# Cross attention and two fp32 MLPs on one core: where the next batch's x, the parts of V and one batch of products stand in the first MLP's steps

## The chip, the core and the metric

The kernel runs on one core of a Trainium2 chip. Five engines matter: TensorE (PE; its weight loads are listed apart as PEld), VectorE (DVE), ScalarE (ACT), GpSimd (POOL) and SyncE (SP), which here does nothing but issue DMA transfers. The metric is the device time of one execution in microseconds (us).

## The reference

Eight batches of attention, and two MLPs over all the tokens of the result. Everything is float32.

```python
B, H, S, Ns, D = 8, 8, 512, 32, 64          # x: (B,H,S,D), state: (B,H,Ns,D)
a  = softmax(x @ state.T / sqrt(D))          # per batch and head, S x Ns
xread = a @ state                            # S rows
a2 = softmax(state @ x.T / sqrt(D))          # Ns x S
sread = a2 @ x                               # Ns rows
X = concat([xread, sread]) -> (B*(S+Ns), H*D) = 4352 x 512
# MLP 1: w_in 512 x 2048, w_out 2048 x 512
h = X @ w_in
g = where(h >= 1, h, where(h <= -1, 0, (h + 1)**2 / 4))
Y = g @ w_out
# MLP 2: its own w_in, w_out of the same sizes, and a slope alpha per hidden unit
h2 = Y @ w_in2
out = (max(h2, 0) + alpha * min(h2, 0)) @ w_out2
```

## The kernel before, in words

A product of float32 matrices is made as a sum of three products of a rounded type: each operand is split into a high part and a rest (names ending in `h` and `l`), and high by high, rest by high and high by rest are added up in one PSUM bank. ACT makes the high part (a cast, L73), DVE the rest (a subtraction, L76).

**The first MLP's steps.** The tokens of batch t make tile t (t = 0 to 7, 512 columns); tile 8 holds the 256 rows of sread. Hidden units come in 16 blocks of 128. One *step* i is one (tile, block) pair; `gi(t, f)` is the number of the step of tile t and block f, so tile 1 is steps 16 to 31, tile 7 is steps 112 to 127. In the turn of step i the source has, one behind the other: the cast and the rest of g of step i+1 (`g_split`: ACT `gh`, DVE `gl`); the side work that tables hang on that step (`at(i, ...)`); `h_mm(i+2)`, the six products that make the hidden block two steps ahead in a PSUM bank `hA` (L84); its activation (ACT `y` L549 and L550, DVE `g` L552); `out_mm(i)`, twelve products into four banks `accA` (L584); and the work hung behind them (`by(i, ...)`). The side work of a tile is the attention of the *next* batch, the decoding of weights for the second MLP, and, in tile 7, the first of the second MLP's inputs. The second MLP (`second()`, lines from L700 on) follows tile 8.

**V.** xread @ w_in is not formed from xread: since xread = a @ state, the kernel makes V = state @ w_in once per batch (PE `vgp`, L460, four batches at a time as a group; ACT copies them to `vgo`, L463), writes V to DRAM (`vd<-vgo`, L475, `vg_store`), and reads each batch's V back in eight parts of 256 KB (`vr_load`, L481: `vr<b><block><half>`). Each part is split: ACT `vw...h` (`vr_hi`, L73), DVE `vw...l` (`vr_lo`). `h_mm` multiplies these by the attention weights `ath` and `atl` (the split of `at`, which the attention of that batch makes). Part (block blk, half q) of batch b is cast by ACT at step o = t0 + 10 + 4 blk + q, t0 being the first step of the tile *before* batch b's own; `vr_load` was hung on o - 2.

**x for the scores.** The scores of batch b are made in tile b-1, from t0 on: `ld_x1` loads x in an order that DVE can transpose (`s0`, L152), `s2_all` multiplies (PE `sc`, L179, at step t0 + 2), then softmax in stages `s3` to `s9` (L189 to L203 and on), with PE transposes `et` (L203). For b > 1 each half q of a batch is 8 transfers of 64 KB, 32 partitions of 128-byte pieces (L130), all hung on one step, t0 + q - 4, into two tiles of 2 KB a partition.

**Who decides the order.** All loads in question go through one queue, SP's, in its order. An engine executes its instructions in the order of its list; that list is laid out ahead of time by a scheduler that takes, among the instructions it believes ready, the one that stands first in the source. So TensorE's list is not the source's: an instruction whose inputs the scheduler holds for late is passed by later ones. Tiles in SBUF come from pools in turn: `U` has 72 buffers of 2 KB a partition, `V` 14 buffers of 4 KB; a load into a buffer that is still read waits, at the head of SP's queue, and what stands behind it waits too. In PSUM four banks serve `hA`, `vgp`, `sc` and `et` in turn, four serve `accA`.

Where the functions below begin with `at` or `by`, the first argument is the step.

Of the kernel before, what the change touches and what calls it, by code (L numbers as in the profile page):

```python
# [40 lines left out]
def kernel_body(ctx: ExitStack, tc: tile.TileContext, x, state, w1i, w1o, w2i, w2o, alpha, out):  # L41
# [9 lines left out]
    def U(name, dt=F32):  # L51
        return up.tile([128, 512], dt, tag="u", name=name)

    def V(name, dt=F32):
        return vp.tile([128, 1024], dt, tag="v", name=name)
# [7 lines left out]
    act, dve, pool, pe, ld = nc.scalar, nc.vector, nc.gpsimd, nc.tensor, nc.sync  # L63

    def run(*calls):


        gens = [g for g in (fn(*a) for fn, *a in calls) if g is not None]
        while gens:
            gens = [g for g in gens if next(g, gens) is not gens]  # L70
# [32 lines left out]
    A = {}  # L103
# [12 lines left out]
            op=ALU.mult)  # L116
        BD[b] = f

    def ld_x1(b, q):
        A[b, q] = {}  # L120
        if b == 1:
            t = A[b, q]["x1"] = V(f"x1_{b}{q}")
            ld.dma_start(out=t, in_=x[b, 4 * q:4 * q + 4].rearrange("h (s r) d -> (h s) (r d)", r=16))
            return
        A[b, q]["x1"] = [U(f"x1_{b}{q}{u}") for u in range(2)]
        for u, t in enumerate(A[b, q]["x1"]):
            for h in range(2):
                for e in range(2):
                    p = 64 * (h ^ q) + 32 * e
                    ld.dma_start(out=t[p:p + 32].rearrange("s (r i) -> s r i", i=32),  # L130
                                 in_=x[b, 4 * q + 2 * u + h, :, 32 * e:32 * e + 32].rearrange("(r s) i -> s r i", s=32))

    def ld_x2(b, q):
# [8 lines left out]
    def s0(b, q):  # L142
        a = A[b, q]
        x1 = a.pop("x1")
        a["xt"] = []
        for e in range(2):
            t = U(f"xt{b}{q}{e}")
            if b == 1:
                dve.transpose(out=t.rearrange("p (s r) -> p r s", r=16),
                              in_=x1.rearrange("p (r e i) -> p r e i", e=2, i=32)[:, :, e, :])  # L150
            else:
                dve.transpose(out=t, in_=x1[e])  # L152
            a["xt"].append(t)
            yield

# [185 lines left out]
    def first_back(q):  # L341
# [4 lines left out]
        a["at"] = ps  # L346

    STAGES = [s0, None, s2, s3, s4, s5, s6, s7, s8, s9]

    W = {}  # L350
# [163 lines left out]
    steps = [(t, f) for t in range(NB + 1) for f in range(NF)]  # L514

    def gi(t, f):
        return t * NF + f
# [6 lines left out]
    def h_mm(i):  # L524
        t, f = steps[i]
        n = wd_(t)
        blk, c = f // 4, (f % 4) * 128
        fs = slice(c, c + 128)
        ps = PS(f"hA{t}{f}")
        if t < NB:  # L530
            terms = []
            for q in range(2):
                vh, vl = VW[t, blk, q]
                ah, al = aT[t, q]
                terms.append((vh[:, fs], vl[:, fs], ah, al))
        else:
            terms = [(W["w1s", blk, k][0][:, fs], W["w1s", blk, k][1][:, fs],
                      XS["h"][:, k * 256:(k + 1) * 256], XS["l"][:, k * 256:(k + 1) * 256]) for k in range(4)]
        mm3(ps[:, :n], terms)
        HP[i] = ps  # L540
# [25 lines left out]
    def out_mm(i):  # L566
        t, f = steps[i]
        n = wd_(t)
        if f == 0:
            for k in range(NO):  # L570
                ACC[k] = pa.tile([128, 512], F32, tag="acc", name=f"accA{t}{k}")
        if i < NAT:

            g, w = GH.pop(i), G["dec", ("w1o", f)]
            for k in range(NO):
                pe.matmul(ACC[k], w[:, k * 128:(k + 1) * 128], g, start=(f == 0), stop=(f == NF - 1))  # L576
            return out_end(i)
        gh, gl = GH.pop(i)
        wh, wl = W["w1o", f]
        for k in range(NO):  # L580
            ks = slice(k * 128, (k + 1) * 128)
            prods = ((wh[:, ks], gh[:, :n]), (wh[:, ks], gl[:, :n]), (wl[:, ks], gh[:, :n]))
            for j, (a, b) in enumerate(prods):
                pe.matmul(ACC[k][:, :n], a, b, start=(f == 0 and j == 0), stop=(f == NF - 1 and j == 2))  # L584
        out_end(i)
# [380 lines left out]
    side = defaultdict(list)  # L966
# [3 lines left out]
    def at(i, fn, *a):  # L970
        side[i].append((fn, *a))

    def by(i, fn, *a):
        behind[i].append((fn, *a))
# [31 lines left out]
    for b in range(1, NB):  # L1006
        t0 = gi(b - 1, 0)
        for q in range(2):
            o = t0 + 4 * q
            n = o if b == 1 else t0 + q - 1  # L1010
            at(n - 2 - (b > 1), ld_x1, b, q)
            at(o + 3, ld_x2, b, q)
            for k, s in enumerate(STAGES):
                if s is s2 and b > 1:
                    if q:
                        at(t0 + 2, s2_all, b)
                elif s:
                    at((n if k == 0 else t0 + q if k == 3 and b > 1 else o) + k, s, b, q)
        for blk in range(4):
            for q in range(2):  # L1020
                o = t0 + 10 + 4 * blk + q
                at(o - 2, vr_load, b, blk, q)
                at(o, vr_hi, b, blk, q)
                at(o + 1, vr_lo, b, blk, q)

# [4 lines left out]
    for blk in range(4):  # L1030
        for c in range(4):
            if blk:
                o = 4 * blk + 1 + c
                at(o, vg_mm, 0, blk, c)
                at(o + 2, vg_store, 0, blk, c)
                o = gi(1, c) if blk < 2 else 4 * blk - 7 + c
                by(o, vg_mm, 1, blk, c)
                if blk > 1:
                    by(o, v0_move, blk, c)
                    if c % 2:  # L1040
                        by(o + 1, vr_hi, 0, blk, c // 2)
                        by(o + 1, vr_lo, 0, blk, c // 2)
                at(o + 2, vg_store, 1, blk, c)
            at(gi(1, 4 * blk + c - 4), wi_store, blk, c)

    for blk in (1, 2, 3):
        for c in range(4):
            o = 4 * blk - 7 + c - (blk > 1)
# [3 lines left out]
    for f in range(1, NF):  # L1052
        o = f - 2 - (f >= NAT)
        at(o - 3, d_load, ("w1o", f), src_w1o(f))
        decode(("w1o", f), o)
    for f in range(NF):
        o = gi(1, f - 3) if f < NAT else f - 2
# [73 lines left out]
    st_build(0)  # L1131
    st_build(1)
    run((s9, 0, 0), (s9, 0, 1), (dec1, ("w1o", 0)))
    for i in range(min(side), len(steps)):
        todo = [(g_split, i + 1)] if 0 <= i + 1 < len(steps) else []
        if i in (-4, -3):
            h_mm(i + 4)
            todo.append((act_fn, i + 4))
        todo += side.pop(i, [])
        if 0 <= i < len(steps) - 2:  # L1140
            h_mm(i + 2)
            todo.append((act_fn, i + 2))
        run(*todo)
        if i >= 0:
            out_mm(i)
        run(*behind.pop(i, []))
    second()


# [27 lines left out]
```

## Time and profile before

| what | us |
|---|---|
| median of 3 runs | 1371.51 (1370.38 to 1373.39) |
| the profiled execution, its own time | 1371.31 |
| its span in the trace | 1369.4 |
| PE busy in the span | 1336.7 |
| tile 1 of the first MLP | 82.57 |
| tiles 2 and 5 | 69.11 and 69.13 |
| tiles 4 and 6 | 72.23 and 72.98 |
| tile 7 | 66.47 |

The span is the stretch of the trace from the first to the last instruction; the execution's own time holds 1.9 us more around it. A tile's time is from its first product into `accA` to that of the next tile. Tiles 1 to 6 have the same arithmetic on PE but for the four pairs of `vgp` products that stand in tile 1 (18 more PE records than in tile 2); tile 7 has no attention to make for a further batch.

### The profile page before, as it was taken

How to read it: one execution, taken by the hardware profiler on the slowest of the kernel's cores; microseconds unless marked ns; L12 is line 12 of the kernel's file. 1: busy time of each engine (PE TensorE's matmuls, PEld its weight loads, DVE VectorE, ACT ScalarE, POOL GpSimd, SP SyncE). 2: the span in 40 equal slices, each digit the busy share in tenths (PEclk: the TensorE clock that was granted, in tenths of full speed). 3: DMA queues.
4: the chain of work that ended last, by engine and by line, in shares of the span. 5: the costliest groups of instructions: out<-in, count | busy, mean ns of one | idle time of the engine just before them, and what ended most of it. 6: DMA issues, size and time to landing. Idle time of an engine off the chain costs nothing.

```text
span 1369.4 us, 20766 instructions
## 1 busy us (share of the span) xinstructions
PE 1336.7 (98%) x6936; PEld 1108.2 (81%) x6936; DVE 1024.9 (75%) x1849; ACT 779.2 (57%) x1500; POOL 75.2 (5%) x94
## 2 busy tenths in 40 slices
PE   6999999999999999999999999999999999999998
PEld 3345668787878787888987888888889999999998
DVE  6897464868777877976978796787858777796873
ACT  4667765666666755766665454444635545464552
POOL 0010000011101120211200000000000000000000
PEclk9999999999999999999999999999999999999999
DMA  6978842265585647376467676656687888869875
GB/s 227 339 241 282 221 132 55 70 162 173 146 229 151 194 125 196 127 244 215 148 223 279 215 277 197 232 155 218 212 258 267 283 286 297 275 239 286 266 263 179
DMA packets 279370, 293.82 MB, mean 215 GB/s; under 512 B 136160, under 2 KB 170208, under 8 KB 279264
## 3 DMA queue, kind: packets, MB, share of 16 engines
q1 hardware_dynamic: 271680, 282.08, 64.8%
q10 hardware_dynamic: 7072, 9.37, 2.1%
q0 software_dynamic: 512, 1.05, 0.3%
q8 instruction: 55, 0.90, 0.3%
q14 instruction: 51, 0.42, 0.1%
HBM read 224.53 MB, written 66.06 MB: 212 GB/s over the span
## 4 chain that ended last, share of the span: by engine, by line
PE 85%; DVE 6%; DMA 5%; ACT 2%; issue 1%; SPq 0%; ACTq 0%; DVEq 0%
PE accB L825 24%; PE hB L750 22%; PE accA L584 21%; PE hA L84 12%; DMA vr<-vd 3%; PE vgp L460 2%; PE accA L576 1%; DMA xr<-xd 1%; PE sr L252 1%; DVE g L552 1%; DMA w1d<-wu 1%; DMA wr_wi<-in_moe_w_in_dram 0%; PE et L203 0%; DMA st<-in_state_dram 0%; DVE c L759 0%
## 5 line engine op out<-in xcount | busy, mean ns | idle before, releaser
L825 PE MATMUL accB<-gs,wv 128*128 128x384 f32 (+1 forms) x1680 | 332.1, 356 | 0.9 <-ACT o L843 0.9
L825 PEld LDWEIGHTS accB<-gs,wv 128*128 128x128 f32 x1680 | 300.9, 188 | 27.5 <-ACT o L843 1.6
L750 PE MATMUL hB<-xh,wu 128*128 128x384 f32 (+1 forms) x1120 | 315.6, 357 | 2.8 <-DVE m L759 1.2
L750 PEld LDWEIGHTS hB<-xh,wu 128*128 128x128 f32 x1120 | 205.7, 188 | 23.6 <-ACT p L776 2.2
L750 PE MATMUL hB<-xl,wu 128*128 128x384 f32 (+1 forms) x560 | 199.6, 356 | 0.0
L73 ACT CAST gs<-c 128x384 fp32r<-128x384 f32 (+1 forms) x200 | 109.3, 557 | 76.3 <-PE accB L825 55.8
L552 DVE SCALAR_TENSOR_TENSOR g<-y,hA 128x512 f32<-128x512 f32 (+1 forms) x144 | 93.6, 650 | 67.1 <-ACT y L550 66.7
L757 ACT ACTIVATE m<-c 128x384 f32<-128x384 f32 (+1 forms) x120 | 68.2, 568 | 118.7 <-DVE c L772 109.3
L76 DVE TENSOR_TENSOR gl<-g,gh 128x512 fp32r<-128x512 f32 (+1 forms) x135 | 93.9, 695 | 47.5 <-ACT gh L73 46.7
L549 ACT ACTIVATE y<-hA 128x512 f32<-128x512 f32 (+1 forms) x144 | 82.5, 573 | 69.2 <-PE hA L84 69.0
L76 DVE TENSOR_TENSOR gs<-c,gs 128x384 fp32r<-128x384 f32 (+1 forms) x200 | 114.6, 603 | 4.4 <-ACT gs L73 3.7
L759 DVE SCALAR_TENSOR_TENSOR c<-m,beta_sb,c 128x384 f32<-128x384 f32 (+1 forms) x120 | 80.9, 674 | 46.5 <-ACT m L757 44.1
L750 PEld LDWEIGHTS hB<-xl,wu 128*128 128x128 f32 x560 | 105.1, 188 | 8.7
L73 ACT CAST gh<-g 128x512 fp32r<-128x512 f32 (+1 forms) x135 | 80.2, 594 | 45.3 <-DVE g L552 37.0
L550 ACT ACTIVATE y<-y 128x512 f32<-128x512 f32 (+1 forms) x144 | 87.5, 608 | 3.8
L799 DVE TENSOR_TENSOR c<-c,c 128x384 f32<-128x384 f32 (+1 forms) x120 | 71.8, 608 | 1.9
L772 DVE TENSOR_TENSOR c<-hB,u 128x384 f32<-128x384 f32 (+1 forms) x80 | 48.5, 606 | 16.5 <-PE hB L750 9.1
L76 DVE TENSOR_TENSOR gs<-m,gs 128x384 fp32r<-128x384 f32 (+1 forms) x80 | 47.1, 608 | 16.4 <-ACT gs L73 16.4
L73 ACT CAST gs<-m 128x384 fp32r<-128x384 f32 (+1 forms) x80 | 43.4, 556 | 24.5 <-PE accB L825 21.1
L463 ACT COPY vgo<-vgp 128x512 f32<-128x512 f32 x64 | 34.8, 588 | 32.2 <-PE vgp L460 31.8
L460 PE MATMUL vgp<-wf_wi,sts 64*128 64x512 f32 x128 | 42.7, 640 | 4.8 <-DVE g L552 3.0
L838 DVE TENSOR_TENSOR c<-accB,o 128x384 f32<-128x384 f32 (+1 forms) x30 | 18.2, 608 | 35.9 <-PE accB L825 28.4
(907 smaller groups left out, 2563.4 us busy)
## 6 DMA issues: line engine op xcount, KB each, us to landing
wu<-w1d SPq DMA_DIRECT2D x280, 256.0 KB
wv<-w2d SPq DMA_DIRECT2D x280, 256.0 KB
vr<-vd SPq DMA_DIRECT2D x56, 256.0 KB
w1d<-wu SPq DMA_DIRECT2D x56, 256.0 KB
w2d<-wo SPq DMA_DIRECT2D x40, 256.0 KB
x<-in_x_dram SPq DMA_DIRECT2D x18, 512.0 KB
wr_wi<-in_moe_w_in_dram SPq DMA_DIRECT2D x16, 512.0 KB
wr_w1o<-in_moe_w_out_dram SPq DMA_DIRECT2D x16, 512.0 KB
```

Of the source, the lines that this page charges most:

```text
L73: act.copy(h, raw)
L76: (eng or dve).tensor_tensor(out=l, in0=raw, in1=h.bitcast(F32), op=ALU.subtract)
L84: pe.matmul(ps, a, b, start=(k == 0), stop=(k == n - 1))
L460: pe.matmul(ps[u], ST[g][rows, c * 128:(c + 1) * 128], w[rows], start=True, stop=True)
L549: act.activation(out=y[:, :n], in_=ps, func=AF.Relu, bias=0.5, scale=0.5)
L550: act.activation(out=y[:, :n], in_=y[:, :n], func=AF.Square)
L552: dve.scalar_tensor_tensor(out=g[:, :n], in0=y[:, :n], scalar=1.0, in1=ps, op0=ALU.min, op1=ALU.max)
L584: pe.matmul(ACC[k][:, :n], a, b, start=(f == 0 and j == 0), stop=(f == NF - 1 and j == 2))
L750: pe.matmul(ps, a[:, kk], b, start=(new and m == 0), stop=(m == 5), skip_group_check=True)
L759: dve.scalar_tensor_tensor(out=g, in0=m, scalar=beta_sb[:, f:f + 1], in1=h, op0=ALU.mult, op1=ALU.add)
L799: dve.tensor_tensor(out=o, in0=x, in1=y, op=op)
L825: pe.matmul(ps, a[:, js], b, start=(new and k == 0 and n == 0), stop=(k == 7 and n == 2), skip_group_check=True)
```

## The change

Four things change. First, x for the scores goes into one tile of 4 KB a partition per half (pool `V`) in place of two of 2 KB (pool `U`), and its transfers, the same 16 per batch of the same 64 KB, hang four a step on steps t0 - 6, t0 - 5 (half 0), t0 - 4, t0 - 3 (half 1), in place of eight on t0 - 4 and eight on t0 - 3. Second, each of V's parts is loaded at o - 3 in place of o - 2. Third, the products that make V of the second group of batches for blocks 0 and 1 (of those hung on `by`, block 1: `vgp110` to `vgp117`) move from behind steps 16 to 19 to behind steps 21 to 24, all in tile 1, and their stores to DRAM with them. Fourth, from step 16 to step 125 TensorE's list is that of the source; the other engines' lists, and TensorE's before and after, are still laid out by the scheduler.

```diff
--- before.py
+++ after.py
@@ -116,18 +116,18 @@
             op=ALU.mult)
         BD[b] = f
 
-    def ld_x1(b, q):
-        A[b, q] = {}
+    def ld_x1(b, q, us=(0, 1)):
+        if 0 in us:
+            A[b, q] = {"x1": V(f"x1_{b}{q}")}
+        t = A[b, q]["x1"]
         if b == 1:
-            t = A[b, q]["x1"] = V(f"x1_{b}{q}")
             ld.dma_start(out=t, in_=x[b, 4 * q:4 * q + 4].rearrange("h (s r) d -> (h s) (r d)", r=16))
             return
-        A[b, q]["x1"] = [U(f"x1_{b}{q}{u}") for u in range(2)]
-        for u, t in enumerate(A[b, q]["x1"]):
+        for u in us:
             for h in range(2):
                 for e in range(2):
                     p = 64 * (h ^ q) + 32 * e
-                    ld.dma_start(out=t[p:p + 32].rearrange("s (r i) -> s r i", i=32),
+                    ld.dma_start(out=t[p:p + 32, u * 512:u * 512 + 512].rearrange("s (r i) -> s r i", i=32),
                                  in_=x[b, 4 * q + 2 * u + h, :, 32 * e:32 * e + 32].rearrange("(r s) i -> s r i", s=32))
 
     def ld_x2(b, q):
@@ -149,7 +149,7 @@
                 dve.transpose(out=t.rearrange("p (s r) -> p r s", r=16),
                               in_=x1.rearrange("p (r e i) -> p r e i", e=2, i=32)[:, :, e, :])
             else:
-                dve.transpose(out=t, in_=x1[e])
+                dve.transpose(out=t, in_=x1[:, e * 512:e * 512 + 512])
             a["xt"].append(t)
             yield
 
@@ -1008,7 +1008,11 @@
         for q in range(2):
             o = t0 + 4 * q
             n = o if b == 1 else t0 + q - 1
-            at(n - 2 - (b > 1), ld_x1, b, q)
+            if b == 1:
+                at(o - 2, ld_x1, b, q)
+            else:
+                for u in range(2):
+                    at(t0 - 6 + 2 * q + u, ld_x1, b, q, (u,))
             at(o + 3, ld_x2, b, q)
             for k, s in enumerate(STAGES):
                 if s is s2 and b > 1:
@@ -1019,7 +1023,7 @@
         for blk in range(4):
             for q in range(2):
                 o = t0 + 10 + 4 * blk + q
-                at(o - 2, vr_load, b, blk, q)
+                at(o - 3, vr_load, b, blk, q)
                 at(o, vr_hi, b, blk, q)
                 at(o + 1, vr_lo, b, blk, q)
 
@@ -1033,7 +1037,7 @@
                 o = 4 * blk + 1 + c
                 at(o, vg_mm, 0, blk, c)
                 at(o + 2, vg_store, 0, blk, c)
-                o = gi(1, c) if blk < 2 else 4 * blk - 7 + c
+                o = gi(1, 5 + c) if blk < 2 else 4 * blk - 7 + c
                 by(o, vg_mm, 1, blk, c)
                 if blk > 1:
                     by(o, v0_move, blk, c)
@@ -1131,7 +1135,7 @@
     st_build(0)
     st_build(1)
     run((s9, 0, 0), (s9, 0, 1), (dec1, ("w1o", 0)))
-    for i in range(min(side), len(steps)):
+    def step(i):
         todo = [(g_split, i + 1)] if 0 <= i + 1 < len(steps) else []
         if i in (-4, -3):
             h_mm(i + 4)
@@ -1144,6 +1148,14 @@
         if i >= 0:
             out_mm(i)
         run(*behind.pop(i, []))
+
+    for i in range(min(side), gi(1, 0)):
+        step(i)
+    with tc.manual_schedule(engines={mybir.EngineType.PE}):
+        for i in range(gi(1, 0), gi(8, -2)):
+            step(i)
+    for i in range(gi(8, -2), len(steps)):
+        step(i)
     second()
```

SP's list around the loads of V's parts for batch 4, block 2 (`vr420`, the half 0), in tile 3. `x1_...` are the loads of x for the scores of batch 5, `w2d` are stores of decoded weights, `x2_50` is x for another stage. Before:

```order
L481 DMA vr410_3594<-vd0_1_81 128x1x512
L130 DMA x1_500_3596<-in_x_dram 32x16x32 x4
L130 DMA x1_501_3597<-in_x_dram 32x16x32 x4
L481 DMA vr411_3644<-vd0_1_81 128x1x512
L130 DMA x1_510_3646<-in_x_dram 32x16x32 x4
L130 DMA x1_511_3647<-in_x_dram 32x16x32 x4
L650 DMA w2d_90<-wo30_3660 128x512
L650 DMA w2d_90<-wo32_3737 256x1x256 x2
L650 DMA w2d_90<-wo33_3795 256x1x256 x2
L137 DMA x2_50_3914<-in_x_dram 128x16x64
L481 DMA vr420_3784<-vd0_2_82 128x1x512
```

The stretch of the same queue up to the same load with the change:

```order
L130 DMA x1_50_3485<-in_x_dram 32x16x32 x4
L650 DMA w2d_90<-wo22_3453 256x1x256 x2
L130 DMA x1_51_3603<-in_x_dram 32x16x32 x2
L481 DMA vr410_3555<-vd0_1_81 128x1x512
L130 DMA x1_51_3603<-in_x_dram 32x16x32 x2
L481 DMA vr411_3601<-vd0_1_81 128x1x512
L650 DMA w2d_90<-wo23_3501 256x1x256 x2
L357 DMA wr_w2o_8_3616<-in_moe2_w_out_dram 128x512
L130 DMA x1_51_3603<-in_x_dram 32x16x32 x4
L650 DMA w2d_90<-wo30_3654 128x512
L357 DMA wr_w2o_9_3726<-in_moe2_w_out_dram 128x512
L481 DMA vr420_3723<-vd0_2_82 128x1x512
```

The 16 loads of x stood in two blocks right ahead of `vr411` and, with five stores, of `vr420`; now they are spread in pieces of two to four over a longer stretch, ten of them ahead of the part `vr410` (four of these before the rows shown).

TensorE's list in tile 1 at the first of the four pairs of `vgp` (the last `accA` product of a step, the pair, the next hidden block). Before, behind step 16:

```order
L584 MATMUL accA13_1569<-gl16_1492,w_w1o_0h_1388 128x512
L584 MATMUL accA13_1569<-gh16_1491,w_w1o_0l_1390 128x512
L460 MATMUL vgp110_1582<-wf_wi_1_0_396,sts1_368 128x512
L460 MATMUL vgp111_1583<-wf_wi_1_0_396,sts1_368 128x512
L84 MATMUL hA13_1590<-ath10_1030,vw100h_1166 128x512
L84 MATMUL hA13_1590<-atl10_1032,vw100h_1166 128x512
```

With the change, behind step 21:

```order
L584 MATMUL accA13_1571<-gl21_1733,w_w1o_5h_1643 128x512
L584 MATMUL accA13_1571<-gh21_1732,w_w1o_5l_1645 128x512
L460 MATMUL vgp110_1809<-wf_wi_1_0_396,sts1_368 128x512
L460 MATMUL vgp111_1810<-wf_wi_1_0_396,sts1_368 128x512
L84 MATMUL hA18_1817<-ath10_1032,vw120h_1626 128x512
L84 MATMUL hA18_1817<-atl10_1034,vw120h_1626 128x512
```

The pair itself is unchanged; it now stands five steps later, ahead of the hidden block of step 24 in place of that of step 19, as `h_mm` runs two steps ahead. The three other pairs move alike.

DVE's list in tile 7. `xr001` is an addition of two tiles of the second MLP's input (L711, it needs the four loads `xr<-xd`), `gl120` the rest that the second product of step 120 needs, `vw730l` and `vw731l` rests of V's parts. Before:

```order
L552 SCALAR_TENSOR_TENSOR g120_6306<-y120_6307,hA78_6285 128x512
L76 TENSOR_TENSOR vw730l_6294<-vr730_6216,vw730h_6292 128x512
L76 TENSOR_TENSOR gl120_6341<-g120_6306,gh120_6340 128x512
L711 TENSOR_TENSOR xr001_6542<-xr011_6544,xr001_6542 128x1024
L552 SCALAR_TENSOR_TENSOR g121_6345<-y121_6346,hA79_6325 128x512
L76 TENSOR_TENSOR vw731l_6335<-vr731_6253,vw731h_6333 128x512
```

With the change:

```order
L552 SCALAR_TENSOR_TENSOR g120_6296<-y120_6297,hA78_6275 128x512
L76 TENSOR_TENSOR vw730l_6284<-vr730_6169,vw730h_6282 128x512
L711 TENSOR_TENSOR xr001_6532<-xr011_6534,xr001_6532 128x1024
L76 TENSOR_TENSOR gl120_6331<-g120_6296,gh120_6330 128x512
L552 SCALAR_TENSOR_TENSOR g121_6335<-y121_6336,hA79_6315 128x512
L76 TENSOR_TENSOR vw731l_6325<-vr731_6208,vw731h_6323 128x512
```

The addition `xr001` has moved ahead of `gl120`; the rest of the order stands.

## Rows read from the trace of the kernel before

**Rows 1.** The page: engine, busy us, share of the span, instructions.

```profile
PE 1336.7 (98%) x6936; PEld 1108.2 (81%) x6936; DVE 1024.9 (75%) x1849; ACT 779.2 (57%) x1500; POOL 75.2 (5%) x94
```

**Rows 2.** Windows of PE, tiles 1, 2, 4, 6, 7: us, busy, clock, DMA.

```profile
158.39:240.96 82.57, 79.01 (x395) 0.98 0.46 127
240.96:310.07 69.11, 69.11 (x377) 1.00 0.43 117
...
379.33:451.56 72.23, 69.93 (x378) 1.00 0.68 184
...
520.69:593.67 72.98, 70.63 (x377) 1.00 0.61 183
593.67:660.14 66.47, 65.84 (x307) 1.00 0.62 203
```

**Rows 3.** Waits of PE in tiles 1, 4, 6, 7: us, times, longest.

```profile
PE vgp L460 <- DVE g L552: 3.0, 2, 1.9
PE accA L584 <- ACT oA L595: 0.5, 1, 0.5
...
PE et L203 <- DVE g L552: 1.8, 1, 1.8
...
PE et L203 <- ACT e L195: 2.4, 1, 2.4
...
PE accA L584 <- DVE gl L76: 0.6, 1, 0.6
```

**Rows 4.** Timeline of ACT: start, us, instruction, idle before and its releaser.

```profile
181.67 0.62 ACT L73 CAST vw121h<-vr 128x512 fp32r<-128x512 f32 x1 [3.02 <-DMA vr<-vd]
...
392.09 0.62 ACT L73 CAST vw420h<-vr 128x512 fp32r<-128x512 f32 x1 [5.79 <-DMA vr<-vd]
...
532.39 0.62 ACT L73 CAST vw620h<-vr 128x512 fp32r<-128x512 f32 x1 [3.58 <-DMA vr<-vd]
```

**Rows 5.** Timeline of SP's queue, tiles 3 and 4, ahead of `vr420`.

```profile
362.35 6.92 SPq L130 DMA_DIRECT2D x<-in_x_dram  x8
...
370.03 6.68 SPq L130 DMA_DIRECT2D x<-in_x_dram  x8
...
381.92 2.83 SPq L481 DMA_DIRECT2D vr<-vd  x1
```

**Rows 6.** Timeline of SP's queue, tile 1, from `vr121` on.

```profile
171.42 4.17 SPq L481 DMA_DIRECT2D vr<-vd  x1
...
177.14 9.16 SPq L475 DMA_DIRECT2D vd<-vgo  x5
```

**Rows 7.** Timeline of PE, a `vgp` pair in tile 1.

```profile
168.07 1.13 PE L460 MATMUL vgp<-wf_wi,sts 64*128 64x512 f32 x4
169.13 0.50 PE L84 MATMUL hA<-ath,vw110h 128*128 128x512 f32 x1
```

**Rows 8.** Window of PE behind the last `vgp` wait, columns as rows 2.

```profile
186.56:189.98 3.42, 3.42 (x11) 0.50 0.47 136
```

**Rows 9.** Timeline of PE, the scores in tile 6.

```profile
527.23 1.04 PE L179 MATMUL sc<-xt,sts 64*32 64x512 f32 x2
528.20 0.50 PE L584 MATMUL accA<-gl,w_w1o_1h 128*128 128x512 f32 x1
```

**Rows 10.** Timeline of DVE and of PE, tile 7, around step 120.

```profile
621.72 0.69 DVE L76 TENSOR_TENSOR gl<-g,gh 128x512 fp32r<-128x512 f32 x1 [0.78 <-ACT gh L73]
627.52 1.23 DVE L711 TENSOR_TENSOR xr<-xr,xr 128x1024 f32<-128x1024 f32 x1 [5.11 <-DMA xr<-xd]
...
626.54 0.39 PE L584 MATMUL accA<-gl,w_w1o_8h 128*128 128x512 f32 x1
```

**Rows 11.** Timeline of DVE and of PE, the edge of tiles 5 and 6.

```profile
508.69 1.22 DVE L76 TENSOR_TENSOR atl<-at,ath 128x512 fp32r<-128x512 f32 x1
...
508.45 0.39 PE L84 MATMUL hA<-ath,vw600h 128*128 128x512 f32 x1
508.68 0.39 PE L84 MATMUL hA<-atl,vw600h 128*128 128x512 f32 x1
```

## The prediction

> **What bounds the kernel now.** I read the page first, and there TensorE: it is busy for 1336.7 us of the 1369.4 us span [rows 1]. Nothing that only makes another engine faster can pay; time is to be had where TensorE stands still, works at half clock, or switches between kinds of products. The next view is therefore windows of TensorE tile by tile [rows 2]. Tile 2 takes 69.11 us and has no idle time: that is what a tile of this arithmetic costs. Tile 4 takes 72.23 us, tile 6 72.98, tile 1 82.57, of which tile 1 has more to do (four pairs of `vgp` products). So 3.12 us are lost in tile 4, 3.87 in tile 6, and in tile 1 something of 13.46. Third, who it waits for there [rows 3]: two `vgp` products of tile 1 wait 3.0 us in all, the transposes `et` wait 1.8 us in tile 4 and 2.4 us in tile 6, each time for `g` on DVE or `e` on ACT. These are small instructions on engines that are far from full, so the fourth view is what held those engines up: ACT, just before, stood for 3.02 us at the cast `vw121h`, 5.79 us at `vw420h` and 3.58 us at `vw620h`, each time for a part of V to arrive [rows 4]. ACT runs its list in order: behind a blocked cast stand the casts `gh`, the activations `y` and the exponentials `e` of the scores, thus DVE's `g` and `gl`, thus the PSUM bank that a `vgp` or `et` needs. The last view says why the part is late. SP spends 6.92 and 6.68 us on two blocks of x for the scores, and the load of `vr420` only comes at 381.92, its cast being wanted at 386.3 (392.09 less the 5.79 of idle time) [rows 4, 5]. In tile 1 the queue is full of stores of V: `vr121` is issued at 171.42 and arrives ten microseconds later, amid five stores that take 9.16 us [rows 6].
>
> **x earlier and thinner, V's parts a step earlier.** No byte and no transfer is added; 16 transfers a batch stay. What moves is their place in SP's list. I counted there, for each part, the steps between the last wait ahead of it in the queue and its cast. A step is 18 products 0.23 us apart (the two starts in [rows 11]), about 4.1 us. For `vr420` the count goes from 3.7 to 4.7, for `vr120` and `vr121` from 3.0 to 5.0 and 4.0, for `vr620` and `vr621` from 1.7 and 2.7 to 4.6 and 3.7. The ACT stalls of 3.02, 5.79 and 3.58 us [rows 4] are 0.7, 1.4 and 0.9 of a step, and for `vr420` the 13.6 us of x in the way are gone besides [rows 5]. So I take these stalls as gone. In tile 4 this gives back all of the 3.12 us over tile 2; the low bound is the 1.8 us of the wait itself [rows 2, 3]. In tile 6 it gives the 2.4 us of wait [rows 3]. The buffer of 4 KB in place of two of 2 KB costs nothing: the transposes read the same 512 columns, and in the list no load of x waits for a reader of its new buffer; its cover is the 6 to 18 steps between issue and transpose, and if a buffer were late, x would stand at the queue's head as before.
>
> **TensorE in source order.** In tiles 1 to 7 the lists differ in three ways. At the tile edges the scheduler had let the first hidden blocks of the next tile pass ahead of `out_mm` in pieces; that order had no wait, and the new one has none unless the attention weights are late, which is a rival below: 0. The scores of tile 6 stood in two pieces with products of another kind between; the first piece holds TensorE for 0.97 us (528.20 less 527.23 [rows 9]), and I take the two pieces to cost one such stretch more than one piece will: 0.9 us. With the wait of 2.4 that makes 3.3 of tile 6's 3.87; the rest is slower restarts that go with them, and I take 3.87, bounds 2.4 and 3.87. The `vgp` pairs move, and each keeps its price: 1.06 us from the pair to the next product [rows 7], about 1.3 with the slower product on each side. Four make 5.2 us, before and after.
>
> **Tile 1.** Of the 13.46 us over tile 2, 5.2 are the pairs, which stay. 3.0 are the two waits [rows 3]; they go, because the casts `vw120h` and `vw121h` no longer hold up ACT, and because the pairs now stand behind step 21, past those casts. Right behind the second wait TensorE shows a granted clock of 0.50, the lower of its two levels, for 3.42 us [rows 8]: at the upper one the same work is 1.71 us, so 1.71 are lost, and go with the wait. 0.5 is a wait for the copy of tile 0's result [rows 3], which stays. The remaining 3.0 (13.46 less 5.2, 3.0, 1.71 and 0.5) are slow starts around these places; I take 1.2 of them as going. Together 5.9; bounds 4.7 (waits and clock alone) and 7.8 (all but the pairs and the 0.5).
>
> **Tile 7, a cost.** DVE's list puts the addition `xr001` ahead of `gl120`. Before, it stood behind it and waited 5.11 us for its loads, and started at 627.52 [rows 10]; TensorE ran on and lost 0.6 us a step later [rows 3]. The loads have no reason to come sooner. So `gl120` would start at 627.52 + 1.15, end near 629.2, and the second product of step 120, at 626.54 before [rows 10], would wait 2.7 us; the 0.6 behind it goes. That would be +2.1; the loads and DVE's turn may shift by some tenths, and I take +1.4, bounds 0 and +3.8 (2.1 and half clock once more at the price of [rows 8]).
>
> **The sum.** −5.9 − 3.1 − 3.9 + 1.4 = −11.5. The profiled execution took 1371.31 us, span and 1.9 us around it, 0.2 below the median of 1371.51. So 1371.3 − 11.5 = 1359.8; I say **1360.0**. With the small ends (4.7, 1.8, 2.4, +3.8) the gain is 5.1 and the time 1366.2; with the large ones (7.8, 3.1, 3.9, 0) it is 14.8 and 1356.5.
>
> **A rule that speaks against it.** The 16 transfers of x move 64 KB each, and eight of them hold SP's queue 6.92 us, 0.87 us apiece [rows 5]. The Trainium skill ("DMA: Bandwidth & Descriptors", section "Rules for kernel authors") would have many small transfers coalesced into one, since under 64 KB one pays mostly overhead. By that rule the change misses the point, since number and size stay; the trace agrees that x is dear in the queue, but shows the loss only where a part stands right behind it, and not in tile 2. So the rule changes the sum only if x gets in another part's way, which is the first rival.
>
> **Rivals.** *The lateness moves to other parts.* x now stands ahead of other parts: `vr511` goes from 3.7 to 2.7 steps, `vr200` and `vr201` from 4.2 and 3.7 to 3.6 and 3.0; `vr321`, `vr401`, `vr530` and `vr700` have 2.7. In tiles 1 and 6, parts with 3.0 and 1.7 steps held ACT for 3.02 and 3.58 us [rows 4]. Against it: parts with 2.7 steps in tile 2 cost TensorE nothing [rows 2]. If three of them each cost as much as tile 4's wait and its after-effects do (1.8 to 3.1 us, say 2), the time is 1366. *Everything over the floor goes, and tile 7 costs nothing*, because its loads come sooner in a calmer queue: 1356.5, the large ends. *Slower: TensorE in source order blocks at the tile edges.* Before, it could pass a product that lacked the second half of the attention weights; in source order it can't, and everything behind waits. The tightest edge is that of tiles 5 and 6: the rest `atl` starts at 508.69 and ends at 509.9, while the hidden block that needs it ran from 508.45 [rows 11] and now comes behind the twelve products of step 93, 2.7 us later, its fifth product at about 512.1. That leaves 2.2 us of slack. There are six edges; each costs what `atl` comes later than that. To eat 11.5 us it must be 4.1 us late (2.2 + 11.5/6) at every edge, and DVE, the engine in question, is busy 75% [rows 1]; against it, the engines that were late are so because of the stalls that go. At 4.7 us late the time is 1375. *The loads don't run ahead*, held at the queue's head by buffers or by what stands there: then only the pairs have moved, tile 4 and tile 6 stay, and with tile 7's cost it is 1371.3 − 3.0 + 2.1, about 1370.
>
> **How the numbers follow.** The forecast 0.62; lateness elsewhere 0.16; all goes 0.11; loads don't run ahead 0.05; blocked edges 0.06. The predicted time is the forecast's. The range 1355 to 1368.5 holds the forecast with its bounds (1356.5 to 1366.2), the second and third and a margin for terms added up wrong; outside are the last two and a few in 100 of the others. About 0.2%, 2.7 us, is what a measurement of this kernel can tell from no change. Faster by more than that: 0.61 + 0.11 + 0.12 = 0.84. Within it: 0.01 of the forecast, 0.03 of the first rival, 0.04 of the unmoved loads, 0.01 of the edges, 0.09. Slower: 0.07, 0.05 of the edges and 0.01 each of the first rival and of the unmoved loads.
>
> **What will show it.** Right, step by step: tiles 4 and 6 at 69 to 69.5 us; no wait of ACT for `vr` over 1 us in tiles 1, 4, 6; no `vgp` wait and no stretch at clock 0.50 in tile 1, which takes about 76.7; a wait of 1 to 3 us at step 120 in tile 7; the stages behind tile 8 unchanged. Wrong: waits of ACT for `vr` in tiles 2, 3 or 5; waits of `hA` for `atl` at the tile edges; or a `vgp` pair that waits behind step 21 as it did behind step 17, because the bank it takes is held by `g` for another reason.

## The result, and the profile after

The changed kernel takes 1359.25 us (median of 4 runs, 1356.6 to 1359.59), the kernel before beside it 1370.95: a ratio of 0.9907, interval 0.9889 to 0.9925. Forecast were 1360.0, in a range of 1355 to 1368.5. The profiled execution took 1359.08 us, its span is 1356.4.

First the windows of TensorE for the changed kernel, one row a tile, 1 to 7, as [rows 2] (length in us, busy us and in brackets the number of TensorE's entries in the trace, granted clock, DMA share and GB/s):

```profile
159.17:234.97 75.80, 75.40 (x394) 1.00 0.66 174
234.97:304.09 69.12, 69.12 (x378) 1.00 0.41 114
304.09:373.20 69.11, 69.11 (x377) 1.00 0.63 169
373.20:442.31 69.11, 69.11 (x377) 1.00 0.69 189
442.31:511.43 69.12, 69.12 (x378) 1.00 0.67 182
511.43:580.54 69.11, 69.11 (x377) 1.00 0.52 160
580.54:647.31 66.77, 65.89 (x308) 1.00 0.60 196
sum 488.14, PE 486.87; mean PE 69.55
```

Tiles 2 to 6 are all at the 69.11 us that tile 2 took before. Tile 1 has lost 6.77 us, tile 4 3.12, tile 6 3.87; tile 3, which stood at 69.26, 0.15; tile 7 has gained 0.30. That is 13.6 us over the seven tiles (501.75 before). Outside them, tile 1 begins 0.78 us later (159.17 as against 158.39), the stretch behind tile 7 is 0.17 shorter (709.09 as against 709.26), and the execution's own time holds 2.7 us beside the span in place of 1.9.

What TensorE waited for in those tiles (us in all, times, longest), where before there were the rows of [rows 3]:

```profile
PE accA L584 <- DVE gl L76: 1.1, 2, 0.9
PE accA L584 <- ACT gh L73: 0.2, 1, 0.2
```

Neither `vgp` nor `et` waits any more. ACT's waits for V's parts were thirteen before, from 0.8 to 5.8 us and 32.3 us in all (155 to 700 us); three of them stand in [rows 4]. They are down to a single one in all seven tiles:

```profile
ACT vw321h L73 <- DMA vr<-vd: 0.4, 1, 0.4
```

SP's queue ahead of `vr420` (the load at 361.84), where two blocks of x took 6.92 and 6.68 us before [rows 5], has x in pieces of two and four:

```profile
341.47 4.13 SPq L130 DMA_DIRECT2D x<-in_x_dram  x4
...
346.87 1.20 SPq L130 DMA_DIRECT2D x<-in_x_dram  x2
348.19 0.56 SPq L481 DMA_DIRECT2D vr<-vd  x1
...
353.90 5.10 SPq L130 DMA_DIRECT2D x<-in_x_dram  x4
...
361.84 0.56 SPq L481 DMA_DIRECT2D vr<-vd  x1
```

And step 120 in tile 7, on DVE and TensorE, as [rows 10]:

```profile
612.56 1.23 DVE L711 TENSOR_TENSOR xr<-xr,xr 128x1024 f32<-128x1024 f32 x1 [4.76 <-DMA xr<-xd]
613.71 0.69 DVE L76 TENSOR_TENSOR gl<-g,gh 128x512 fp32r<-128x512 f32 x1
...
613.18 0.39 PE L584 MATMUL accA<-gh,w_w1o_8h 128*128 128x512 f32 x1
614.45 0.50 PE L584 MATMUL accA<-gl,w_w1o_8h 128*128 128x512 f32 x1 [0.88 <-DVE gl L76]
```

The addition stands ahead of `gl120` and waits 4.76 us; TensorE's second product of the step then waits 0.88 us. The loads had landed earlier than before with respect to TensorE: before, the addition began 0.98 us after that product (627.52 and 626.54 [rows 10]); now it began 0.85 us before the product's turn (613.18 + 0.23 = 613.41). They were not issued earlier: the last of the four was issued 10.9 us ahead of the product before (615.6) and 9.3 us ahead of its turn now (604.1). What became shorter is the time from that issue to the addition: 11.9 us before, 8.5 now.

### The profile page after: what moved, and what is told of

Same layout as the page of the kernel before. It is cut to its first block, busy times and chain, and to the rows that moved or that the text cites. A ratio compares the mean times of both kernels' runs of the same rounds, so it can differ in the third digit from the quotient of the medians.

```text
span 1356.4 us, 20698 instructions
## 1 busy us (share of the span) xinstructions
PE 1331.5 (98%) x6936; PEld 1107.2 (82%) x6936; DVE 1025.2 (76%) x1849; ACT 780.6 (58%) x1500; POOL 76.3 (6%) x94
## 4 chain that ended last, share of the span: by engine, by line
PE 89%; DVE 4%; DMA 4%; ACT 2%; issue 1%; SPq 0%; ACTq 0%; DVEq 0%; POOL 0%
PE accB L825 24%; PE accA L584 24%; PE hB L750 22%; PE hA L84 13%; PE vgp L460 2%; PE accA L576 1%; DMA vr<-vd 1%; DMA xr<-xd 1%; PE sr L252 1%; DMA wr_wi<-in_moe_w_in_dram 0%; DMA vr<-vgo 0%; PE et L203 0%; PE sc L179 0%; ACT vgo L463 0%; DMA st<-in_state_dram 0%
## 5 line engine op out<-in xcount | busy, mean ns | idle before, releaser
L783 ACT COPY u<-hB 128x384 f32<-128x384 f32 (+1 forms) x40 | 21.0, 524 | 41.8 <-PE hB L750 41.8
```

## The experiments

Total times of one kernel scatter by 2 to 8 us from run to run, so kernels are compared by the tiles in their traces, one traced execution each. All tiles, in us from the first `accA` product of a tile to that of the next, with the ratio of the total times to those of the kernel before, run beside it:

| kernel | 1 | 2 | 3 | 4 | 5 | 6 | 7 | sum | ratio (interval) |
|---|---|---|---|---|---|---|---|---|---|
| before | 82.57 | 69.11 | 69.26 | 72.23 | 69.13 | 72.98 | 66.47 | 501.8 | 1 |
| changed | 75.80 | 69.11 | 69.11 | 69.11 | 69.11 | 69.11 | 66.77 | 488.1 | 0.9907 (0.9889 to 0.9925) |
| no_x | 75.83 | 69.11 | 69.11 | 70.32 | 69.11 | 69.11 | 66.03 | 488.6 | 0.9916 (0.9895 to 0.9936) |
| no_v | 76.36 | 69.11 | 74.09 | 69.69 | 69.11 | 70.34 | 66.87 | 495.6 | 0.9951 (0.9937 to 0.9965) |
| no_g | 76.03 | 69.11 | 69.11 | 69.11 | 69.11 | 69.11 | 66.47 | 488.1 | 0.9898 (0.9878 to 0.9917) |
| no_o | 75.56 | 69.11 | 69.11 | 69.11 | 69.11 | 69.11 | 66.92 | 488.0 | 0.9904 (0.9883 to 0.9925) |
| only_x | 75.62 | 69.11 | 71.43 | 70.94 | 69.11 | 70.55 | 66.83 | 493.6 | 0.9925 (0.9899 to 0.9951) |
| only_v | 76.06 | 69.34 | 68.89 | 70.25 | 68.66 | 69.64 | 66.73 | 489.6 | 0.9905 (0.9876 to 0.9933) |
| only_g | 83.32 | 69.11 | 69.37 | 72.29 | 69.11 | 72.43 | 66.91 | 502.5 | 1.0026 (1.0011 to 1.0041) |
| only_o | 82.53 | 69.11 | 71.34 | 75.48 | 69.11 | 71.31 | 66.05 | 504.9 | 1.0021 (1.0007 to 1.0036) |
| only_v4 | 85.22 | 72.11 | 71.49 | 72.11 | 72.08 | 70.20 | 65.55 | 508.8 | 1.0047 (1.0029 to 1.0064) |
| vo4 | 82.40 | 69.11 | 69.11 | 69.11 | 69.11 | 69.11 | 65.55 | 493.5 | 0.9958 (0.9943 to 0.9972) |
| xr13 | 75.79 | 69.11 | 69.11 | 69.11 | 69.11 | 69.11 | 65.55 | 486.9 | 0.9894 (0.9865 to 0.9924) |
| xv13 | 75.96 | 69.11 | 69.11 | 69.11 | 69.11 | 69.11 | 65.55 | 487.1 | 0.9894 (0.9875 to 0.9912) |

Where the scheduler lays out TensorE's list, a window can hold some hidden products of the next tile or lack some, at 0.23 us each. The number of entries shows it: in only_v tile 4 has 383 in place of some 377, tiles 5 and 6 have 376 and 375; in only_v4 tile 1 has 406 in place of some 394, tile 6 has 367. There the sum over the tiles is the safer figure. Behind tile 7 all fourteen executions take 709.0 to 709.3 us, so nothing hides there.

### One part undone

**no_x**: x loaded as before; the other three parts stay.

```diff
-            if b == 1:
-                at(o - 2, ld_x1, b, q)
-            else:
-                for u in range(2):
-                    at(t0 - 6 + 2 * q + u, ld_x1, b, q, (u,))
+            at(n - 2 - (b > 1), ld_x1, b, q)
... (ld_x1 and the transposes as in the kernel before)
```

> The change without its first part: x for the scores loaded as before (eight transfers on each of two steps, 2 KB buffers), V's parts three steps ahead, the moved pairs and TensorE's order kept. Theory A (late parts of V stall ACT and through it TensorE; x's blocks are one reason, the place of the loads the other): in SP's list the sixteen loads of x now stand as one block right ahead of vr420 and of vr620, so 13.6 us of queue lie ahead of them, but they are issued about a step earlier than before; vr620 counts 4.3 steps from the last wait ahead of it, vr420 4.2. A expects ACT waits at vw420h of 0 to 2 us instead of 5.8, and TensorE to lose 0 to 2 us in tiles 4 and 6 together: 1359 to 1361. Rival B (x in the queue is the whole cause, the step of V's loads none): tiles 4 and 6 come back to 72.2 and 73, 1366. Rival C (TensorE's order is what brings it): as the changed kernel, 1359.

It lost 1.2 us in tile 4 and nothing elsewhere (tile 7 is 0.7 us shorter). B falls, A held; C is not settled by a total of 1360.56 us, but by no_o below. The loss is not a late part (no wait of ACT for a part is over 0.6 us): sixteen loads of x stand in the queue from 354.32 to 367 in this run, and right behind them, at the edge to tile 4, ACT took 5.2 us to issue three of its own stores.

**no_v**: V's parts two steps ahead again.

```diff
-                at(o - 3, vr_load, b, blk, q)
+                at(o - 2, vr_load, b, blk, q)
```

> The change without its second part: V's parts two steps ahead again; x spread, pairs moved, TensorE in source order. Theory A: vr420 counts 2.7 steps, vr620 2.7, vr120 and vr121 3.0, with four or no loads of x near them; ACT waits for parts come back in part, 1 to 3 us at several casts, and TensorE loses 0 to 4 us in tiles 1, 4 and 6. The addition xr001 stands behind gl120 again, so the wait of 0.9 us at step 120 goes. 1358.5 to 1363. Rival B (x is the whole cause): 1358.5, tiles 4 and 6 at 69.1. Rival D (the step of the loads is the whole cause): tiles 4 and 6 back at 72 to 73, 1365.

The seven tiles lost 7.4 us, more than half of the gain, 4.98 of it in tile 3, which no theory had named. The total, 1365.43 us, is over A's range of 1358.5 to 1363, and tile 7 did not get shorter as A had it. The waits of ACT in this run:

```profile
ACT vw321h L73 <- DMA vr<-vd: 5.7, 1, 5.7
...
ACT vw320h L73 <- DMA vr<-vd: 4.0, 1, 4.0
ACT vw421h L73 <- DMA vr<-vd: 3.4, 1, 3.4
ACT vw121h L73 <- DMA vr<-vd: 3.1, 1, 3.1
ACT vw621h L73 <- DMA vr<-vd: 3.0, 1, 3.0
```

Late parts are back, but partly at other parts: spreading x without loading V's parts earlier moves the lateness. B falls, and D in its numbers (tile 4 did not come back). A wait of ACT does not cost TensorE its whole length: before, ACT stood 3.9 us at `vw321h` and tile 3 lost 0.15 us; here it stood 3.1 us at `vw121h` and tile 1 lost 0.56.

**no_g**: the `vgp` pairs behind steps 16 to 19.

```diff
-                o = gi(1, 5 + c) if blk < 2 else 4 * blk - 7 + c
+                o = gi(1, c) if blk < 2 else 4 * blk - 7 + c
```

> The change without its third part: the four pairs of vgp products behind steps 16 to 19 as before. Theory A: the pairs waited because ACT stood at vw120h and vw121h; these parts now have 5.0 and 4.0 steps, so no wait over 0.5 us, no half clock, tile 1 within 0.7 us of 75.8: 1359. Rival E (the pairs' place is what counts, since behind steps 16 to 19 the banks are held by the scores and the hidden blocks): two waits of 1 to 2 us are back and with them perhaps the half clock, tile 1 at 79 to 82.5: 1362 to 1366.

**no_o**: the loop as before, TensorE's list left to the scheduler.

```diff
-    def step(i):
+    for i in range(min(side), len(steps)):
...
-    for i in range(min(side), gi(1, 0)):
-        step(i)
-    with tc.manual_schedule(engines={mybir.EngineType.PE}):
-        for i in range(gi(1, 0), gi(8, -2)):
-            step(i)
-    for i in range(gi(8, -2), len(steps)):
-        step(i)
```

> The change without its fourth part: TensorE's list laid out by the scheduler throughout. With x spread, this list differs from the source's only in step 17 (two hidden products and two accA products placed earlier); the scores of tile 6 stand in one piece without it. Theory A: as the changed kernel within 0.5 us, 1359. Rival C (the source order is what brings the gain): 1366 or more.

Both give the changed kernel's tiles, tile 1 within 0.25 us. Given the other parts, neither the place of the pairs nor TensorE's order does anything.

### One part alone

The same four edits, each alone on the kernel before.

> The kernel before with the second part alone: V's parts three steps ahead. Theory A, as the first four runs narrowed it (the step at which V's parts are loaded does nearly all; place of the pairs and TensorE's order nothing): waits of ACT for parts under 1.5 us each, the vgp pairs behind steps 16 to 19 wait at most 0.7 us, tile 1 at 76 to 77, tile 4 at 69.1 to 70.4, tile 6 at 69.1 and up to 0.9 more for the scores, which stand in pieces of one and seven here; tile 7 about 66.8. In all 9 to 12 us under the kernel before. Rival B2 (x's blocks and the place of the loads only work together): 4 to 7 us under it, with ACT waits of 2 to 4 us left.

Earlier parts of V alone give 12.2 of the 13.6 us. The windows of tiles 1, 4 and 6, and ACT's only wait for a part:

```profile
162.36:238.41 76.05, 75.09 (x394) 1.00 0.43 123
...
376.64:446.89 70.25, 70.25 (x383) 1.00 0.66 182
...
515.55:585.19 69.64, 69.64 (x375) 1.00 0.61 188
...
ACT vw621h L73 <- DMA vr<-vd: 0.6, 1, 0.6
```

No wait for `vgp` or `et` is left. Tile 4 is over 69.11 only by the five hidden products more that stand in its window (1.14 us at 0.23 each). The scores of tile 6 stand in pieces of one and seven here; its window is 0.5 us over 69.11 although it holds three hidden products fewer, so the second piece costs about 1.2 us by this estimate (0.5 and three times 0.23).

> The kernel before with the first part alone: x spread and earlier, V's parts two steps ahead. Theory A: late parts stay late and only change place: ACT waits of 3 to 6 us at parts of tile 3 (vr320 counts 1.7 steps as against 2.6), 1 and 6; tile 3 at 71 to 74, tile 4 at 69 to 70, tile 6 at 69 to 71, tile 1 at 78 to 83. In all 0 to 6 us under the kernel before. Rival B (x is the cause): tiles 3, 4 and 6 at 69.1 and 7 us or more under it.

8.2 us by the tiles: more than A allowed and as much as B had, but B's tiles (3, 4 and 6 at 69.1) did not come. Tiles 3 and 6 are as A had them (ACT waits 5.9 us at `vw321h`), tile 4 is 0.9 us over A's bound (4.6 at `vw421h`); A was wrong on tile 1, which is all the way at 75.62. The load of `vr120` tells why; in this kernel it was issued at

```profile
154.97 1.80 SPq L481 DMA_DIRECT2D vr<-vd  x1
```

with the tile beginning at 157.66. Before, the load was not issued until 161.96 and then took 4.55 us of the queue, behind sixteen loads of x and eight stores of the very V that it reads back; there the tile began at 158.39:

```profile
140.30 7.04 SPq L130 DMA_DIRECT2D x<-in_x_dram  x8
...
148.12 6.50 SPq L130 DMA_DIRECT2D x<-in_x_dram  x8
154.72 4.56 SPq L475 DMA_DIRECT2D vd<-vgo  x8
...
161.96 4.55 SPq L481 DMA_DIRECT2D vr<-vd  x1
```

So in tile 1 x's blocks were in the way too, of the stores.

> The kernel before with the third part alone: the vgp pairs behind steps 21 to 24. Theory A2 (the pairs' move is a second remedy for the same stall in tile 1, since the run without V's earlier loads had the 3.1 us wait of ACT at vw121h and yet a tile 1 of 76.4): the 3.0 us waits of ACT at vw120h and vw121h stay, but no vgp product waits over 0.5 us and no half clock follows, tile 1 at 76 to 77; tiles 4 and 6 as before at 72.2 and 73. 5 to 7 us under the kernel before. Rival (in tile 1 only the time of the parts counts): tile 1 at 80 to 82.6.

A2 fell. ACT still stood, 4.84 us each at `vw120h` and `vw121h`, and the wait simply came out at another product, the transposes `et`, longer than the two `vgp` waits of [rows 3]:

```profile
PE et L203 <- ACT e L195: 4.9, 1, 4.9
```

> The kernel before with the fourth part alone: TensorE in source order from step 16 to 125. Theory A: the stalls of ACT for parts stay, tile 4 at 72 to 73, tile 1 at 80 to 83; the scores of tile 6 stand in one piece, tile 6 at 72 to 72.5. 0 to 2 us off the kernel before, to either side. Rival C (source order brings it): 5 us or more under it.

C fell. The scores of tile 6 are whole and tile 6 is 1.7 us shorter, but the late parts cost more elsewhere:

```profile
ACT vw321h L73 <- DMA vr<-vd: 6.8, 1, 6.8
...
ACT vw420h L73 <- DMA vr<-vd: 6.1, 1, 6.1
```

Tiles 3 and 4 lost 2.1 and 3.3 us against the kernel before, where ACT stood 3.9 and 5.8 us at the same two casts. In tile 4 TensorE's granted clock was 0.50 from 406.8 to 410.0, behind a wait of 2.9 us at `et`. A had tile 4 at 72 to 73 and did not name tile 3, so it missed both. Why `vr321` comes later in this order no run shows.

### How far ahead

**only_v4**: the kernel before with V's parts loaded at o - 4.

```diff
-                at(o - 2, vr_load, b, blk, q)
+                at(o - 4, vr_load, b, blk, q)
```

> The kernel before with V's parts loaded four steps ahead in place of two, all else as before. Theory A (how far ahead V's parts are loaded decides; one step, as in the second part alone, gave nearly all): no ACT wait for a part over 0.5 us in tiles 1 to 6, and the rest of what the second part alone left goes where it came from parts: tiles 1 to 6 within 0.5 us of the second part alone or of the floor of 69.1, in all as the second part alone or up to 1 us less. Rival X (x, now behind the parts in the queue, comes too late itself and DVE waits at its transposes): waits of DVE for x of 1 to 3 us in tiles 3 to 6, one or two tiles 1 to 3 us over the second part alone.

There is no wait of ACT at a cast of V's parts, as A says, and none of DVE for x, against X; and yet the kernel is slower than the one before, which both theories missed. Two things took the place of the old waits. The windows of tiles 1, 2 and 4:

```profile
160.49:245.71 85.22, 78.87 (x406) 0.96 0.47 134
245.71:317.82 72.11, 71.80 (x378) 1.00 0.42 115
...
389.31:461.42 72.11, 71.80 (x378) 1.00 0.62 169
```

and the timeline of TensorE, the wait in tile 1 and the scores of tile 3:

```profile
167.82 0.80 PE L584 MATMUL accA<-gh,w_w1o_0h 128*128 128x512 f32 x1 [5.68 <-ACT oA L595]
...
320.86 1.06 PE L179 MATMUL sc<-xt,sts 64*32 64x512 f32 x8
...
323.95 0.49 PE L584 MATMUL accA<-gl,w_w1o_1h 128*128 128x512 f32 x1 [0.91 <-DVE gl L76]
...
325.99 1.06 PE L179 MATMUL sc<-xt,stx 64*32 64x512 f32 x8
```

x now stands behind V's parts, and the scores stand in two or three pieces among `accA` products (in the trace 4 and 4 products in tile 3, each product two of the rows' entries, and 1, 3 and 4 in tiles 2, 4, 5 and 6). A piece takes 1.04 to 1.06 us however few products it holds: eight in one piece take 1.1 us, below. That the scheduler splits them because it holds x for late is argued; that its order is what splits them the next run shows. In tile 1 TensorE waits 5.68 us for the copy of tile 0's result, which ACT makes late: between its issues of the stores `xd<-oA` ACT stood for most of 5.9 us.

**vo4**: the same with TensorE in source order.

> V's parts four steps ahead as in the run before that was slower than the kernel before, with the fourth part of the change on top (TensorE in source order from step 16 to 125). Theory F (in the run before, tiles 2 to 6 took 70.2 to 72.1 us because the scheduler, with x late behind V's parts, put the scores into two or three pieces among products of another kind, about 1 us for each piece more; and tile 1 took 85.2 because a copy of tile 0's result waited 6.2 us for the queue): the scores stand in one piece, no wait of TensorE for them, tiles 2 to 6 at 69.1 to 69.6; tile 1 keeps the wait of 5.7 us and stays at 81 to 85; 10 to 12 us under the run before. Rival (x itself is late, and TensorE in source order must wait where the scheduler worked around it): waits of TensorE for the scores' transposes of 1 to 3 us in tiles 2 to 6, and no gain.

F held for tiles 2 to 6, to the hundredth; the gain over the run before, 15.3 us by the tiles, is more than its 10 to 12. The windows of tiles 2, 3 and 4, with 5 and 6 the same:

```profile
240.87:309.99 69.12, 69.12 (x378) 1.00 0.45 116
309.99:379.10 69.11, 69.11 (x378) 1.00 0.61 172
379.10:448.21 69.11, 69.11 (x377) 1.00 0.66 182
```

and in the timeline of TensorE the scores of tile 3:

```profile
318.24 0.63 PE L179 MATMUL sc<-xt,sts 64*32 64x512 f32 x4
...
318.72 0.61 PE L179 MATMUL sc<-xt,stx 64*32 64x512 f32 x4
```

The scores of tile 3 stand in one piece from 318.24 to 319.33, and no wait of TensorE is listed in tiles 2 to 6. Of the 15.3 us by which the seven tiles shrank 12.4 lie in the windows of tiles 2 to 6; of the 2.8 in tile 1 about 2.7 are the twelve entries more that its window held in only_v4. Tile 1 keeps a wait of 4.4 us for that copy.

### A version that goes on from there

**xr13**: the changed kernel, the second MLP's first input loaded a step later.

```diff
-        at(gi(7, 12), xr_load, 0, k % 2, k // 2)
+        at(gi(7, 13), xr_load, 0, k % 2, k // 2)
```

**xv13**: the same on the first two parts alone (`no_g` and `no_o` together, and this line).

> The changed kernel with the second MLP's first input loaded one step later (behind step 125 in place of 124, by the table), by which DVE's list puts the addition xr001 between the rests of steps 123 and 124, four steps later. The loads then have 5.0 and 3.9 steps from the last wait in the queue to the addition. Theory A: the wait of 0.9 us at step 120 goes and none takes its place: tile 7 at 65.8 to 66.1 in place of 66.8, 0.7 to 1.0 us under the changed kernel, too small for the clock of a whole run and to be read in the trace. Rival: the loads come later too, and DVE stands before gl124 as it stood before gl120: tile 7 at 66.5 to 68.

> The first two parts alone (x spread, V's parts three steps ahead), with the pairs and TensorE's order as before, and the second MLP's first input loaded one step later. Theory A (the third and fourth parts bring nothing): tiles 1 to 6 as in the changed kernel within 0.5 us, tile 7 at 65.5 to 66 in place of 66.8, so 1 us under the changed kernel from tile 1 to tile 7. Rival: the third and fourth cover for each other, and without both a wait of 1 us or more is back in tile 1 or at a tile edge.

The tile 7 of xv13:

```profile
578.40:643.95 65.55, 65.55 (x308) 1.00 0.61 199
```

Without a gap, 1.2 us under the changed kernel, in both; the other tiles are its tiles within 0.2 us. Both rivals fell. So the third and fourth parts do not cover for each other, and the first two with this line are as fast by the tiles as all four with it (487.1 and 486.9, the lowest sums). In the time of a whole run 1.2 us cannot be told (0.9894 as against 0.9907, the intervals overlap).

## Why the prediction was right, and where it was not

**What bounds, and the cause.** Right. TensorE's waits came from ACT's casts, these from the parts, and with the parts in time (only_v) TensorE's waits for `vgp` and `et` are gone; where parts are late (no_v, only_x, only_g, only_o) it waits again, in no_v and only_x in tile 3 too, which had lost only 0.15 us before.

**Tiles 4 and 6.** −3.12 and −3.87 forecast and measured, all of the loss over tile 2. What a second piece of scores costs was taken as 0.9 us; a piece holds TensorE for 1.0 us in only_v4 (320.86 to 321.85, 325.99 to 326.99), and in only_v the second one costs about 1.2.

**Tile 1.** −5.9 forecast, −6.77 measured, within the bounds of 4.7 and 7.8: of the 3.0 us of slow starts more went than the 1.2 taken. But one of the two reasons given there was wrong, that the waits go "because the pairs now stand behind step 21, past those casts". With the parts late (only_g) the wait goes to `et` and tile 1 grows by 0.75 us; with the parts in time (no_g) the old place costs nothing.

**Tile 7, the term that was mis-sized.** +1.4 forecast, +0.30 measured. The mechanism stands, with its engine, line and step. The step that was off is "The loads have no reason to come sooner": the working took them to land where they had landed before, and so made the wait 2.7 us; it was 0.88, as they landed 1.8 us sooner with respect to the step (0.98 after, 0.85 before the product's turn). With the old wait of 0.6 gone, 0.88 is the +0.30. The prediction had given the shift half a sentence ("may shift by some tenths"). The trace shows that the last load took 3.5 us less from its issue to the addition, though it was issued later with respect to the step; why it took less is not shown.

**How much each part brings.** The prediction summed by place and did not divide by part. The runs divide: V's parts earlier 12.2 us alone, x spread 8.2 alone, 13.6 together; the two overlap, since each alone mends tile 1 and most of tile 6 (tile 4 only the first does in full; x alone gives 1.3 of its 3.12 us and costs 2.2 in tile 3). The others bring nothing beside them, and by themselves cost about 0.2%. On top of only_v4, though, the fourth part is worth 15.3 us, 12.4 of them in tiles 2 to 6: it keeps the scores whole where the scheduler would split them.

**The rivals.** Lateness that moves to other parts did not happen in the changed kernel (one wait of 0.4 us), but did in no_v and only_x, at `vr320` and `vr421`, with `vr321` later than before. No wait for `atl` at a tile edge appears, so the slack of 2.2 us held. The rule of the Trainium skill on many small transfers ("DMA: Bandwidth & Descriptors", section "Rules for kernel authors") was not put to the test: number and size stayed in every run, and the 13.6 us came from their place and that of V's loads alone.

**The sum.** Tiles −13.6 us, start +0.8, behind tile 7 −0.2, by the spans −13.0; by the profiled executions −12.2 and by the medians −11.7, as against −11.5 forecast. The two mis-sized terms, 1.1 us in tile 7 and 0.9 in tile 1, both made the gain too small, by 2.0 us; 0.8 before tile 1 and 0.8 beside the span went the other way. That the forecast met the median within a microsecond owes something to that.

## What to carry to other kernels

An engine that executes in order and starts a block of its work with a cast of something loaded is only as early as that load; count, in the list of the queue, the steps from the last wait ahead of the load to its use, and compare with what the trace shows that it takes. Earlier is not better without end: a load that goes ahead pushes another behind it, and a scheduler that holds the other for late will rearrange the busiest engine's list around it; look at that list again after each such move. When several edits mend the same wait, undo each and do each alone before any of them is called the cause.

## What was not expected of the hardware

**The clock at the start.** Executions differ before tile 1. In the traced execution of the changed kernel TensorE's granted clock fell between 25 and 35 us; in that of xv13 it did not. Windows of TensorE, 25 to 30 and 30 to 35 us, of the changed kernel:

```profile
25.00:30.00 5.00, 3.18 (x12) 0.75 0.88 335
30.00:35.00 5.00, 4.33 (x12) 0.57 0.03 12
```

and of xv13:

```profile
25.00:30.00 5.00, 2.19 (x13) 1.00 1.02 391
30.00:35.00 5.00, 4.95 (x20) 1.00 0.59 225
```

Tile 1 began at 159.17 and 156.88 us in these. In six of the fourteen traced executions (the changed kernel, only_v, only_g, only_o, only_v4, xr13) the clock from 30 to 35 us is 0.50 to 0.57, and tile 1 begins at 159.2 to 162.5 us; in the other eight it is 0.91 to 1.00, and tile 1 begins at 156.9 to 158.9. The kernel before is among the eight, and the 0.78 us by which its tile 1 begins earlier may be no more than this. The one run of the changed kernel whose mean clock was 1.000 took 1356.6 us, the three at 0.997 took 1359.1 to 1359.6. Why the clock falls in one execution and not in another no run shows, and with one trace a kernel it is not shown either that the clock alone makes the difference of up to 5.6 us.

**ACT held at its own stores.** In no_x, only_v4 and vo4, where sixteen loads of x stand late in SP's queue, ACT stood for 5.2 to 5.9 us between its issues of `xd<-oA`, on another queue; in the other eleven such a group of issues took at most 2.8 us. In no_x:

```profile
371.65 5.22 ACTq L600 DMA_DIRECT2D xd<-oA  x3
376.91 0.62 ACT L73 CAST gh<-g 128x512 fp32r<-128x512 f32 x1 [5.16 <-DMA xd<-oA]
```

The changed kernel differs from no_x in x's loads alone and took 1.94 us for the same three issues (at 372.05), so in no_x the place of x's loads brings this about. It is not enough by itself: in only_v, with x loaded as in no_x, the issues took 1.98 us. What ACT waited for there the traces do not show.
